# The first chunk's attention in fixed slots on TensorE

## The chip, the cores and the metric

One Trainium2 chip, of which the kernel uses one core. The metric is the device time of one execution in microseconds (us). The kernel before took 813.23 us as the median of three runs (812.15 to 815.35).

## The reference

Attention whose queries and keys meet only where a hash of both is the same, followed by two feed-forward layers:

```python
# q, k, v: (2, 8, 768, 64); proj: (64, 6)
q_bits = (einsum('bhsd,dk->bhsk', q, proj) > 0)
k_bits = (einsum('bhsd,dk->bhsk', k, proj) > 0)
mask = q_bucket[:, :, :, None] == k_bucket[:, :, None, :]
scores = where(mask, q @ k.T / sqrt(64), -1e9)
attn = exp(scores - max); attn /= sum(attn) + 1e-9
x = heads joined of attn @ v                   # (1536, 512)
h = maximum(x @ w_in, 0);  x = (h * h) @ w_out     # first layer, d_ff 2048
h = x @ w_in2; x = (maximum(h, 0) + alpha * minimum(h, 0)) @ w_out2
```

The weights arrive as float64 bits and are converted to float32 on the chip.

## The kernel before, in words

The 1536 rows are cut into four chunks of 384 (T). The attention of chunk 0 runs alone at the start (`attention(0, 2)`); that of chunks 1 to 3 (`attention_beside`) runs in the background of the first layer's matmuls (`feed_forward`) of chunks 0 to 2. The second layer follows (`wide_hidden`, `whole_project`).

In a chunk the eight heads go in four pairs (`Pair`), one head in each half of the partitions. A pair has six units: head h, query block t of 128 rows. `scores` (L382) makes four matmuls into a buffer of `s_tile` (two buffers, `s` and `acc`, that alternate), DVE takes the maximum of 768 scores (`low`, L393) and ACT the exponent with its sum (`sm`, L396). `p_t` (L403) transposes the result on TensorE, three key blocks to a bank of `m_tile`, and evicts it to `pt` on ACT (L415) or DVE (L417), by the letters of `EVICT`. `av` (L419) multiplies six key blocks by the values, two matmuls (one per head, each into half of the columns) a block; the trace shows two records for each of these. `recip` (L437) turns the sums into a row and spreads it over the partitions by way of DRAM, or, for the last pair of chunk 0, by matmuls (`spread`, L461); `finish` (L471) multiplies and splits into a high and a low part for the feed-forward layer.

A pair is prepared while the one before runs: `k_bits` and `q_split` hash on TensorE (L239), `matches` compares hash codes on TensorE (L255), `k_split` makes high and low parts of the keys, `k_ids` makes the key row that is zero where a code matches (L279, DVE), and two DMAs each bring these into the tile `k` (L275, L285). `q_halves` (L306) and `q_yes` (L326) do the same for the queries. The first pair is prepared in one piece, `at_once` (L331).

In chunk 0 `m_tile` hands out three PSUM banks in turn (two of `ps_m` and `ps_h`), for transposes, hashes, matches and products alike. `pt` has two buffers, one for each head of a pair, so that a pair's first transposes wait for the products of the pair before. In the order of the program, two preparation steps follow each score group, and the six blocks of products follow the last transposes of a pair. That order is only a priority: a planner lists the instructions of each engine by what it takes to be ready first. `tc.keep_in_program_order` binds an instruction to the written order on its engine; before, `Pair.next` used it for some instructions of the first two pairs. Behind the attention of chunk 0, `fetch` converts the first feed-forward weights (DVE L617, L618, L623; ACT L615), allowed to begin after the last unit of pair 2.

Of the kernel before, what the change touches and what calls it, by code (L numbers as in the profile page):

```python
# [17 lines left out]
NEG = -(2.0 ** 100)  # L18
# [11 lines left out]
def kernel(  # L30
# [64 lines left out]
    p2 = pool("p2", 2, att)  # L95
    p4 = pool("p4", 4, att)
    sm3 = pool("sm3", 3, att)

# [31 lines left out]
    pop = const.tile([P, 1], F32, name="pop")  # L130
    off = const.tile([P, 1], F32, name="off")

    def constants():
# [3 lines left out]
        with tc.tile_pool(name="once", bufs=1) as once:  # L137
# [32 lines left out]
            first(nc.vector.tensor_scalar(off, pop, -1.0, 1.0, ALU.mult, ALU.add))  # L170
# [35 lines left out]
    class Pair:  # L206
# [26 lines left out]
        def hash_bits(self, x, n):  # L233
# [4 lines left out]
            for g in range(NG):  # L238
                self.next(nc.tensor.matmul(  # L239
# [6 lines left out]
        def matches(self, bits, n):  # L246
# [6 lines left out]
            for g in range(NG):  # L253
                a, k = divmod(g * w, T)
                nc.tensor.matmul(ps[:, a, k:k + w], code[:, g, :], bits, start=True, stop=True)  # L255
# [35 lines left out]
        def q_split(self):  # L291
# [6 lines left out]
            self.q3 = p1.tile([P, 3, T], F32R, tag="q3", name="q3")  # L298
# [17 lines left out]
        def q_ids(self):  # L316
# [4 lines left out]
            nc.scalar.activation(self.q3[:, 0], y[:, 0, :], AF.Relu, bias=off)  # L321
# [4 lines left out]
        def q_yes(self, y):  # L326
            for h in range(2):
                r, o = self.rows(h)
                self.next(nc.scalar.activation(self.q[o, h, 0], y[r, 0, :], AF.Relu, bias=off[r]))

        def at_once(self):  # L331
# [10 lines left out]
            for h in range(2):  # L342
                self.next(nc.scalar.activation(q[r[h], h, 0], self.qn[r[h]], AF.Copy, scale=scale))
            nc.gpsimd.tensor_copy(k[r[0], 0, 1], f32(k[r[0], 0, 0]))
            nc.gpsimd.tensor_copy(q[o[0], 0, 1], f32(q[r[0], 0, 0]))
            nc.sync.dma_start(out=f32(k[r[1], 1, 1]), in_=f32(k[r[1], 1, 0]))
            nc.sync.dma_start(out=f32(q[o[1], 1, 1]), in_=f32(q[r[1], 1, 0]))
            k_y = self.matches(k_bits, S)
            for h in range(2):
# [136 lines left out]
    def attention(c, lag):  # L486
# [33 lines left out]
        while late:  # L520
            tail()
# [688 lines left out]
```

## Time and profile before

| | us |
|---|---|
| median of three runs | 813.23 |
| lowest, highest | 812.15, 815.35 |
| profiled execution | 814.07 |
| its span | 812.3 |
| TensorE matmuls busy | 773.7 (95%) |
| DVE, ACT, GpSimd busy | 541.5, 507.1, 317.1 |

The profile is of one execution. Busy is the time in which an engine has an instruction under way; a matmul's record includes the time until its results are out, so that records that follow each other overlap. "idle before <- releaser" is the time for which an engine did nothing ahead of an instruction and the work that ended that wait. Times of a row count from the span's start.

### The profile page before, as it was taken

To read this page: it belongs to the slowest core of one execution; us is meant where nothing else is said; L and a number is where in the kernel's file an instruction comes from. 1 tells how busy PE (TensorE), PEld (TensorE's weight loads), DVE (VectorE), ACT (ScalarE), POOL (GpSimd) and SP (SyncE) were. 2 spreads that over 40 slices of the span, in tenths; PEclk is the share of its full clock that TensorE was granted. 3 is DMA by queue.
4 is the path that set the end of the run, shared out by engine and by line. 5 is a ranking of instruction groups with operands and counts; after the bars stand their busy time and mean duration, and the time that the engine had idled before them with its cause. 6 is when DMAs were issued, how large, how long until landed. Compare 5 with 4: busy or idle time off the path is not lost.

```text
span 812.3 us, 12536 instructions
## 1 busy us (share of the span) xinstructions
PE 773.7 (95%) x4330; PEld 634.4 (78%) x4330; DVE 541.5 (67%) x876; ACT 507.1 (62%) x988; POOL 317.1 (39%) x231
## 2 busy tenths in 40 slices
PE   6899899999999998999999999999999999999998
PEld 4565777766778676676867769999999888999886
DVE  8578899887756657788977964574667622766111
ACT  5678778767565555565756656775777633777331
POOL 1012322233346464654343342002558354558440
PEclk9999999999999999999999999999999999999999
DMA  6856878778678586768785657451321226511222
GB/s 179 216 160 207 270 244 253 240 218 247 167 247 237 178 246 216 249 231 272 221 268 160 223 198 284 123 162 44 133 71 53 56 68 206 193 58 57 65 65 91
DMA packets 56708, 143.67 MB, mean 177 GB/s; under 512 B 7402, under 2 KB 11652, under 8 KB 56644
## 3 DMA queue, kind: packets, MB, share of 16 engines
q1 hardware_dynamic: 56644, 142.87, 56.4%
q8 instruction: 34, 0.56, 0.3%
q14 instruction: 30, 0.25, 0.1%
HBM read 96.62 MB, written 25.47 MB: 150 GB/s over the span
## 4 chain that ended last, share of the span: by engine, by line
PE 47%; DVE 4%; DMA 3%; issue 1%; ACT 1%; ACTq 0%; DVEq 0%
PE b L1036 5%; PE b L1037 5%; PE b L1042 5%; PE b L903 5%; PE b L902 5%; PE b L904 5%; DMA wf<-w 3%; PE m L427 2%; PE s L388 1%; PE h L706 1%; PE h L707 1%; PE h L708 1%; PE m L411 1%; PE acc L751 1%; PE acc L747 1%
## 5 line engine op out<-in xcount | busy, mean ns | idle before, releaser
L668 POOL TENSOR_TENSOR wl<-wf,wh 128x512 fp32r<-128x512 f32 x64 | 88.6, 1387 | 80.4 <-ACT wh L667 74.8
L939 POOL TENSOR_TENSOR wp<-wraw,wp 128x1024 fp32r<-128x1024 f32 (+1 forms) x32 | 68.3, 2136 | 117.7 <-ACT wp L936 96.0
L667 ACT ACTIVATE wh<-wf 128x512 fp32r<-128x512 f32 x128 | 79.8, 628 | 54.4 <-PE h L707 23.1
L396 ACT ACTIVATE sm<-s,low 128x768 f32<-128x768 f32 x84 | 75.6, 900 | 49.4 <-DVE low L393 49.2
L719 POOL TENSOR_TENSOR gl<-g,gh 128x384 fp32r<-128x384 f32 x48 | 54.6, 1137 | 128.9 <-ACT g L716 65.0
L393 DVE TENSOR_REDUCE low<-s 128x1 f32<-128x768 f32 x84 | 80.0, 952 | 31.0 <-PE s L388 30.8
L388 PE MATMUL s<-k,q 128*128 128x384 f32 x336 | 80.8, 360 | 10.7 <-ACT sm L396 9.5
L411 PE MATMUL m<-ident,sm 128*128 128x128 f32 x531 | 85.3, 277 | 5.9 <-DVE pt L417 3.3
L411 PEld LDWEIGHTS m<-ident,sm 128*128 128x128 f32 x531 | 65.4, 142 | 24.1 <-DVE pt L417 4.9
L1026 POOL TENSOR_TENSOR gp<-g,gp 128x768 fp32r<-128x768 f32 x32 | 63.2, 1981 | 50.5 <-ACT gp L1023 50.5
L388 PEld LDWEIGHTS s<-k,q 128*128 128x128 f32 x336 | 58.2, 193 | 27.8 <-ACT sm L396 17.5
L706 PE MATMUL h<-xh,wh 128*128 128x384 f32 x212 | 77.2, 364 | 2.1 <-DVE u L474 1.7
L1036 PE MATMUL b<-wp,gp 128*128 128x512 f32 x192 | 75.0, 391 | 0.0
L904 PE MATMUL b<-xph,wp 128*128 128x384 f32 x224 | 74.8, 334 | 0.0
L902 PE MATMUL b<-xph,wp 128*128 128x384 f32 x224 | 74.8, 334 | 0.0
L903 PE MATMUL b<-xpl,wp 128*128 128x384 f32 x224 | 74.8, 334 | 0.0
L1037 PE MATMUL b<-wp,gp 128*128 128x512 f32 x192 | 74.8, 389 | 0.0
L708 PE MATMUL h<-xh,wl 128*128 128x384 f32 x212 | 71.9, 339 | 0.3 <-POOL wl L668 0.3
L707 PE MATMUL h<-xl,wh 128*128 128x384 f32 x212 | 71.7, 338 | 0.0
L668 DVE TENSOR_TENSOR wl<-wf,wh 128x512 fp32r<-128x512 f32 x64 | 48.2, 757 | 31.2 <-ACT wh L667 31.2
L1020 DVE TENSOR_TENSOR wp<-wp 128x512 fp32r<-128x512 f32 x28 | 25.4, 911 | 64.0 <-ACT wp L1017 64.0
L427 PE MATMUL m<-pt,vr 128*64 128x384 f32 x336 | 66.2, 498 | 1.5 <-DVE rrow L445 0.9
(180 smaller groups left out, 1824.4 us busy)
## 6 DMA issues: line engine op xcount, KB each, us to landing
wf<-w SPq DMA_DIRECT2D x96, 256.0 KB, 3.1
wbits<-in_w_in_dram SPq DMA_DIRECT2D x32, 512.0 KB, 4.3
wbits<-in_w_out_dram SPq DMA_DIRECT2D x32, 512.0 KB, 4.0
wraw<-ws SPq DMA_DIRECT2D x16, 896.0 KB, 4.7
q<-q SPq DMA_DIRECT2D x48, 192.0 KB, 3.9
w<-wf SPq DMA_DIRECT2D x32, 256.0 KB, 2.2
wp<-w SPq DMA_DIRECT2D x32, 256.0 KB, 2.6
k<-kh SPq DMA_DIRECT2D x14, 384.0 KB, 6.3
```

The source lines that it names most:

```text
L388: nc.tensor.matmul(ps[:, a, 0:HALF], self.q[:, h, i, qs], self.k[:, h, i, ks], start=i == 0, stop=i == 1)
L393: low_ins = nc.vector.tensor_reduce(low, ps[:, 0:2, 0:HALF], AX.XY, ALU.max, negate=True)
L411: nc.tensor.transpose(ps[:, i * P:(i + 1) * P], pp[:, b * P:(b + 1) * P], ident)
L427: nc.tensor.matmul(self.o[r, 0:T], self.vr[:, b, r], self.pt[h][:, :, b, :], start=(b == 0), stop=(b == NKB - 1),)
L668: engine.tensor_tensor(lo, w, f32(hi), ALU.subtract)
L706: nc.tensor.matmul(hp, wih[:, ks], xh[:, kk, :], start=first, stop=False)
L708: nc.tensor.matmul(hp, wil[:, ks], xh[:, kk, :], start=False, stop=last)
L902: nc.tensor.matmul(ps, w[0][:, ms], gh, start=first, stop=False, skip_group_check=True)
L903: nc.tensor.matmul(ps, w[0][:, ms], gl, start=False, stop=False, skip_group_check=True)
L904: nc.tensor.matmul(ps, w[1][:, ms], gh, start=False, stop=last, skip_group_check=True)
L1036: nc.tensor.matmul(a, g[:, 0, b], w[:, 0], start=f == 0, stop=False)
L1037: nc.tensor.matmul(a, g[:, 0, b], w[:, 1], start=False, stop=False)
```

## The change

For chunk 0 the steps are written out by `attention_first` in 24 slots. Slot n holds the scores of unit n, one step of the next pair's preparation (in pair 0 from the second slot on), the transposes of unit n - 2 (and the sums' row after a pair's last), and key blocks of the products of the pair before: one block in slot 1, two in slots 2 and 3, one in slot 4; `finish` of that pair is in slot 5. After the last slot the last pair's products follow in three groups of two blocks. All matmuls of chunk 0's attention are bound to this order (`Pair.pe`). The products take `ps_h` (`h_tile`) and all else the two banks of `ps_m`. `pt` has a third buffer (`third`), used for every third head; its memory later serves `y` and the second chunk's `q3`. The key row becomes 0 or -1 (a sign on ACT in the first pair, in `at_once`, with the order of the steps there changed; DVE elsewhere), and the factor 2^100 goes to the query's row.

```diff
     def m_tile():
         state["m"] += 1
-        if not state["moe"] and state["m"] % 3 == 0:
-            return ps_h.tile([P, 512], F32, tag="h", name="h")
         return ps_m.tile([P, 512], F32, tag="m", name="m")
...
+        def pe(self, ins):
+            if self.c == 0:
+                tc.keep_in_program_order(ins)
...
-                self.kr[:, 0].bitcast(F32R).rearrange("p (a n) -> p a n", n=T), y, pop, NEG,
+                self.kr[:, 0].bitcast(F32R).rearrange("p (a n) -> p a n", n=T), y, pop, -1.0,
                 ALU.not_equal, ALU.mult,
...
-            self.q3 = p1.tile([P, 3, T], F32R, tag="q3", name="q3")
+            self.q3 = state["q3"].tile([P, 3, T], F32R, tag="q3", name="q3")
...
-            for h in range(2):
-                self.next(nc.vector.tensor_tensor(k[o[h], h, 1], kr[r[h]], f32(k[r[h], h, 0]), ALU.subtract))
-                if h == 0:
-                    self.q_yes(self.matches(self.hash_bits(self.qn, T), T))
-                self.next(nc.vector.tensor_scalar(
-                    k[o[h], h, 0].rearrange("p (a n) -> p a n", n=T), k_y[r[h]], pop[r[h]], NEG,
-                    ALU.not_equal, ALU.mult,
-                ))
...
+            def ids(h):
+                self.next(nc.scalar.activation(
+                    k[o[h], h, 0].rearrange("p (a n) -> p a n", n=T), k_y[r[h]], AF.Sign, bias=npop[r[h]]
+                ))
...
+            low("k", 0)
+            q_bits = self.hash_bits(self.qn, T)
+            q_y = self.matches(q_bits, T)
+            ids(0)
+            self.next(nc.scalar.activation(q[r[1], 1, 0], self.qn[r[1]], AF.Copy, scale=scale))
             nc.sync.dma_start(out=f32(q[o[1], 1, 1]), in_=f32(q[r[1], 1, 0]))
+            low("q", 0)
+            yes(0)
+            ids(1)
+            low("k", 1)
+            low("q", 1)
+            yes(1)
...
-                self.pt[h] = p2.tile([P, NTB, NKB, P], F32, tag="pt", name="pt")
+                by = "third" if self.c == 0 and (2 * self.j + h) % 3 == 2 else "p2"
+                self.pt[h] = state[by].tile([P, NTB, NKB, P], F32, tag="pt", name="pt")
...
-            if part == 0:
-                self.o = m_tile()
             n = NKB // 3
-            for b in range(part * n, (part + 1) * n):
+            self.blocks(part * n, (part + 1) * n)
+
+        def blocks(self, b0, b1):
+            if b0 == 0:
+                self.o = h_tile() if self.c == 0 else m_tile()
+            for b in range(b0, b1):
...
+    def attention_first():
+        units, lag = 2 * NTB, 2
+        pairs = [Pair(0, j) for j in range(NPAIR)]
+        for step in pairs[0].prepare():
+            step()
+        prep = []
+
+        def turn(n):
+            pr, u = pairs[n // units], n % units
             for a in range(2):
+                pr.p_t(*divmod(u, NTB), a)
+            if u == units - 1:
+                pr.recip()
+
+        parts = {1: (0, 1), 2: (1, 3), 3: (3, 5), 4: (5, 6)}
+        for n in range(NPAIR * units):
+            j, u = divmod(n, units)
+            if u == 0 and j + 1 < NPAIR:
+                prep = pairs[j + 1].prepare()
+            pairs[j].scores(*divmod(u, NTB))
+            if prep and (u or j):
+                prep.pop(0)()
+            if n >= lag:
+                turn(n - lag)
+            if j and u in parts:
+                pairs[j - 1].blocks(*parts[u])
+            if j and u == units - 1:
+                pairs[j - 1].finish()
+            assert not (prep and u == units - 1)
+        for n in range(NPAIR * units - lag, NPAIR * units):
+            turn(n)
+        for b in range(0, NKB, 2):
+            pairs[-1].blocks(b, b + 2)
+        pairs[-1].finish()
...
     state["moe"] = True
+    passing.close()
+    state["y"] = pool("y", 1, layer1, side="right")
+    state["q3"] = pool("q3", 1, passing, side="right")
     wide_banks.close()
```

## Rows read from the trace of the kernel before

**Rows 1.** Busy time by stage: length, engines (instructions), clock, DMA share, GB/s.

```profile
core 0: us, PE busy (x) PEld busy (x) DVE busy (x) ACT busy (x) POOL busy (x), PEclk, DMA share, GB/s
8.40:24.90 16.50, 13.55 (x73) 10.04 (x73) 12.62 (x17) 10.51 (x21) 1.77 (x2) 1.00 0.73 174
24.90:43.10 18.20, 16.62 (x114) 10.44 (x112) 12.12 (x21) 11.72 (x27) 1.62 (x2) 1.00 0.66 182
43.10:60.40 17.30, 16.05 (x108) 10.38 (x108) 12.21 (x21) 12.91 (x29) 2.07 (x3) 1.00 0.69 187
60.40:74.20 13.80, 13.21 (x76) 8.54 (x76) 11.68 (x22) 11.23 (x25) 2.85 (x2) 1.00 0.58 180
74.20:86.00 11.80, 8.91 (x62) 5.16 (x62) 11.34 (x22) 8.77 (x18) 3.22 (x5) 1.00 0.74 259
86.00:497.00 411.00, 392.61 (x2262) 302.41 (x2262) 316.08 (x512) 262.31 (x532) 168.87 (x139) 1.00 0.74 231
```

**Rows 2.** Waits of TensorE, 86 to 497 us: sum, times, longest.

```profile
PE s L388 <- ACT sm L396: 6.9, 8, 1.8
```

**Rows 3.** Waits of ACT and DVE, 24.8 to 60.3 us: sum, times, longest.

```profile
ACT u L435 <- PE m L427: 4.8, 1, 4.8
ACT u L435 <- PE h L427: 4.3, 1, 4.3
...
DVE low L393 <- PE acc L388: 7.1, 5, 3.7
```

**Rows 4.** TensorE's timeline, slots without products: start, length, instruction, count.

```profile
58.68 0.94 PE L388 MATMUL acc<-k,q 128*128 128x384 f32 x4
...
60.35 0.97 PE L388 MATMUL s<-k,q 128*128 128x384 f32 x4
61.16 0.82 PE L411 MATMUL m<-ident,sm 128*128 128x128 f32 x6
61.99 0.97 PE L388 MATMUL acc<-k,q 128*128 128x384 f32 x4
...
70.02 0.82 PE L411 MATMUL m<-ident,sm 128*128 128x128 f32 x6
70.60 0.94 PE L388 MATMUL acc<-k,q 128*128 128x384 f32 x4
```

**Rows 5.** TensorE's timeline, the last pair's products and what follows each group.

```profile
78.92 2.80 PE L427 MATMUL m<-pt,vr 128*64 128x384 f32 x16 [0.34 <-ACT pt L415]
81.65 0.93 PE L465 MATMUL h<-rrow,pick 6*128 6x128 f32 x6
82.51 1.51 PE L427 MATMUL m<-pt,vr 128*64 128x384 f32 x8
83.95 0.37 PE L239 MATMUL m<-qn,proj_sb 128*32 128x96 f32 x8
```

**Rows 6.** TensorE's timeline, a pair's key hash and key matches.

```profile
25.74 0.53 PE L239 MATMUL h<-kr,proj_sb 128*32 128x192 f32 x8
...
46.64 0.49 PE L255 MATMUL acc<-bits,code 128*128 128x192 bf16 x4
```

**Rows 7.** Timelines of DVE, ACT and TensorE in the first 18 us.

```profile
9.87 1.02 DVE L353 TENSOR_SCALAR k<-s,pop 64x768 fp32r<-64x768 f32 x1
...
12.50 0.90 ACT L396 ACTIVATE sm<-acc,low 128x768 f32<-128x768 f32 x1 [3.53 <-DVE low L393]
...
15.94 1.48 PE L388 MATMUL s<-k,q 128*128 128x384 f32 x4
```

**Rows 8.** Pair 1's key identities, issue on SP; landing times of that line.

```profile
16.29 2.45 SPq L285 DMA_DIRECT2D k<-kr  x2
...
DMA to landing us min/median/max: 4.8/5.9/7.1
```

**Rows 9.** Timelines at the end of the stage: last scores, last multiplication, first feed-forward matmul.

```profile
74.19 0.96 PE L388 MATMUL acc<-k,q 128*128 128x384 f32 x4
...
85.38 0.55 DVE L474 TENSOR_TENSOR u<-u,h 128x384 f32<-128x384 f32 x1
...
85.98 0.44 PE L706 MATMUL h<-xh,wh 128*128 128x384 f32 x1 [1.66 <-DVE u L474]
```

More of the change, by code (lines that the diff above doesn't have):

```diff
@@ L94 @@
     p1 = pool("p1", 1, att)
-    p2 = pool("p2", 2, att)
+    p2 = state["p2"] = pool("p2", 2, att)
     p4 = pool("p4", 4, att)
     sm3 = pool("sm3", 3, att)
+    passing = ctx.enter_context(ExitStack())
+    state["third"] = pool("third", 1, passing, side="right")
     def s_tile():
@@ L169, in constants @@
             first(nc.vector.tensor_reduce(pop, ones, AX.X, ALU.add))
-            first(nc.vector.tensor_scalar(off, pop, -1.0, 1.0, ALU.mult, ALU.add))
+            first(nc.vector.tensor_scalar(npop, pop, -1.0, None, ALU.mult))
+            first(nc.vector.tensor_scalar(off, pop, -FAR, FAR, ALU.mult, ALU.add))
     xT = {}
@@ L238, in hash_bits @@
             for g in range(NG):
-                self.next(nc.tensor.matmul(
+                self.pe(nc.tensor.matmul(
                     ps[g * GR:(g + 1) * GR, 0:w], proj_sb.rearrange("p h n -> p (h n)"), x[:, g * w:(g + 1) * w],
@@ L320, in q_ids @@
                 return
-            nc.scalar.activation(self.q3[:, 0], y[:, 0, :], AF.Relu, bias=off)
+            nc.scalar.activation(self.q3[:, 0], y[:, 0, :], AF.Relu, bias=off, scale=FAR)
             for h in range(2):
@@ L328, in q_yes @@
                 r, o = self.rows(h)
-                self.next(nc.scalar.activation(self.q[o, h, 0], y[r, 0, :], AF.Relu, bias=off[r]))
+                self.next(nc.scalar.activation(self.q[o, h, 0], y[r, 0, :], AF.Relu, bias=off[r], scale=FAR))
         def at_once(self):
@@ L341, in at_once @@
                 self.next(nc.scalar.activation(k[r[h], h, 0], kr[r[h]], AF.Copy))
-            for h in range(2):
-                self.next(nc.scalar.activation(q[r[h], h, 0], self.qn[r[h]], AF.Copy, scale=scale))
             nc.gpsimd.tensor_copy(k[r[0], 0, 1], f32(k[r[0], 0, 0]))
+            nc.sync.dma_start(out=f32(k[r[1], 1, 1]), in_=f32(k[r[1], 1, 0]))
+            self.next(nc.scalar.activation(q[r[0], 0, 0], self.qn[r[0]], AF.Copy, scale=scale))
             nc.gpsimd.tensor_copy(q[o[0], 0, 1], f32(q[r[0], 0, 0]))
-            nc.sync.dma_start(out=f32(k[r[1], 1, 1]), in_=f32(k[r[1], 1, 0]))
@@ L347, in at_once @@
[L347 to L359 removed]
+            k_y = self.matches(k_bits, S)
@@ new lines, in yes @@
+            def yes(h):
+                self.next(nc.scalar.activation(
+                    q[o[h], h, 0], q_y[r[h], 0, :], AF.Relu, bias=off[r[h]], scale=FAR
+                ))
+            low("k", 0)
[3 more added lines that the diff above has]
+            self.next(nc.scalar.activation(q[r[1], 1, 0], self.qn[r[1]], AF.Copy, scale=scale))
+            nc.sync.dma_start(out=f32(q[o[1], 1, 1]), in_=f32(q[r[1], 1, 0]))
+            low("q", 0)
@@ L484, in new_x @@
         return xT[key]
-    def attention(c, lag):
-        def begin():
-            if (c, 0) not in raw:
-                load_pair(c, 0)
-        pairs = [Pair(c, j) for j in range(NPAIR)]
-        steps = [begin] + pairs[0].prepare()
-        late = []
-        ended = []
-        def tail():
-            pr, h, t = late.pop(0)
-            for a in range(2):
-                steps.append(lambda a=a: pr.p_t(h, t, a))
-            if t == NTB - 1 and h == 1:
-                steps.append(pr.recip)
-                for part in range(3):
-                    steps.append(lambda part=part: pr.av(part))
-                ended.append(pr)
-        for j, pr in enumerate(pairs):
-            nxt = pairs[j + 1].prepare() if j + 1 < NPAIR else []
-            for u in range(2 * NTB):
-                h, t = divmod(u, NTB)
-                steps.append(lambda pr=pr, h=h, t=t: pr.scores(h, t))
-                late.append((pr, h, t))
-                for _ in range(2 if c == 0 else 1):
-                    if nxt:
-                        steps.append(nxt.pop(0))
-                if ended and u == 3:
-                    steps.append(ended.pop().finish)
-                if len(late) > lag:
-                    tail()
-        while late:
-            tail()
-        while ended:
-            steps.append(ended.pop(0).finish)
-        return steps
@@ L1055 @@
     constants()
-    for step in attention(0, 2):
-        step()
+    attention_first()
     with tc.issue_after(keyed[0, 1].ins):
```

38 lines of the change are left out of this document (22 added, 16 removed).

## The prediction

> **What bounds the kernel now.** I read four views, in this order. First the busy time by stage [rows 1], cut where the attention of the first chunk passes from one head pair to the next. Call its 24 score groups n0 to n23: six per pair, one for each head and each block of 128 query rows. n0 starts at about 8.4, n6 at 24.9, n12 at 43.1, n18 at 60.4, n23 at 74.2, and the first feed-forward matmul at 86.0 us. So the stage that the diff rewrites takes 77.6 us, a tenth of the span. Behind it, from 86 to 497 us, TensorE is busy 392.6 of 411.0 us, and its longest kind of wait sums to only 6.9 us [rows 2]: there TensorE's work sets the pace, and a microsecond won before 86 should arrive at the end. In the stage itself DVE and ACT are busy 12 to 13 of some 18 us per pair. Neither is the bound as an average, and TensorE's 16 of 17 to 18 is not either, since its records overlap and include matmuls that run at the wrong time.
>
> What is wrong there shows in the second and third view. TensorE runs the products of a whole pair (24 records, two per matmul) nearly in one piece, and while it does so no new scores come. ACT waits 4.8 and 4.3 us in single stretches for the end of those products, and DVE waits 7.1 us for scores, all between 24.8 and 60.3 us [rows 3]. The fourth view, TensorE's timeline, gives the prices of its pieces: scores take 0.81 us from their start to the next instruction, six transposes 0.57 [rows 4], 16 product records 2.73 and 8 records 1.44 [rows 5].
>
> **The change, part by part, and its sum.** The sum is made against the profiled execution: 814.07 us, of which 812.3 is the span and 1.77 lies around it; this execution is 0.84 above the median of the three, 813.23.
>
> *Slots for pairs 1 and 2.* A slot is now fixed: scores, one step of the next pair's preparation, the six transposes of two slots back, and zero, one or two of the six key blocks of the pair before. TensorE's work for a pair is six times 0.81 + 0.57, 8.28 us. For the products, 16 records (four key blocks) cost 2.73 and 8 records (two blocks) 1.44, so a block costs 0.645 and each group a fixed 0.15; six blocks in four groups (1, 2, 2, 1) cost 4.47. The preparation: the key hash 0.53 and the key matches 0.49 [rows 6]; the query's two have half the columns, so they lie between nothing and these, and I take 0.4 together, towards the upper row since short matmuls do not shrink in proportion. The transposed sums, 0.2 by the same reasoning. In all 14.4 us. On the other side stands the loop through two score buffers: n17 at 58.68, n19 in the same buffer at 61.99, so 3.31 us for two slots [rows 4], 9.9 us for six, which lies below 14.4 and so does not bind on average. It binds in the slots without products (the last of a pair and the first of the next): they have 1.4 to 1.9 us of TensorE work where the loop wants 1.65, and ACT has there the exponent and two query rows of the next pair ahead of evictions. I add 1.1 us a pair for that, between nothing and 2.2. So 15.5 against 18.2 and 17.3 [rows 1]: 2.7 and 1.8 us won.
>
> The products become more groups, and here a rule of the Trainium skill speaks against the change: "TensorEngine Tiling (Array Packing)", Key Properties, says that a change of tiling mode drains TensorE, and the products use a 128 by 64 mode among 128 by 128 matmuls. The trace has the drain in its numbers: the fixed 0.15 us of a group, which makes four groups 0.45 dearer than one. By the rule alone nothing more is due, and the sum holds it.
>
> *The third transposed tile and the bank of its own for products.* They let the first transposes of a pair be written before the products of the pair before have ended. They add no instruction. The price: transposes, hashes and matches lose one of three PSUM banks. I cost that at nothing, because scores (0.81) and products (1.44) stand between two uses of a bank and cover an eviction; where the cover is gone, it is the rival "slower" below.
>
> *Pair 3.* It has no preparation, so n18 to n23 is five times 1.38 plus 4.47 plus 0.2, 11.6 us; with 0.8 us of waits 12.4 against 13.8: 1.4 won.
>
> *The start.* DVE made both key rows of the first pair (1.02 us each), so that ACT waited 3.53 us for the first minimum and started the exponent at 12.50 [rows 7]. Signs on ACT take two 1 us pieces off DVE while ACT waits, so the first exponent can come about 1.1 us sooner. But the preparation of pair 1 now goes one step to a slot, beginning at slot 1, and its key identities stand behind n3 instead of n1. Before, the transfers that bring them were issued from 16.29 for 2.45 us, landing 4.8 to 7.1 us after an issue [rows 8], and n6 came at 24.9. After: n0 at 8.4; scores here run at half speed (1.48 for four in the record at 15.94 [rows 7] against 0.97 for those at 60.35 [rows 4]); three scores, a hash and six transposes at that speed and one wait for an exponent put n3 at about 15.7 us. Its own 1.5, the matches, DVE's minimum and the 1 us identities follow: 19.5. Two issues, which no longer wait behind DVE, 1.2 (half of 2.45): 20.7. Landed at 25.5 to 26.6, and I take 26.0. TensorE keeps its order, so it stands still from about 23 to 26 with n6 at the head of its queue and the transposes of slots 4 and 5 behind it. 1.1 us lost, between 0.5 won and 2.6 lost. In pairs 2 and 3 the identities stand in slot 2, four slots ahead of their scores: some 10 us against the 9 that the same chain takes, so these should just land in time.
>
> *The tail.* Scores, transposes and products behind n23 are the same work in the same order. The first feed-forward matmul waited for the bank of which the last multiplication read (85.38, 0.55 long, behind weight conversions) [rows 9]; that bank now comes free with the copy of the products, about 1 us sooner, but the last third of that group still needs the last pair's columns. 0.8 won, between 0.3 and 1.5.
>
> *Smaller edits.* The query tile of the second chunk waits for the third tile's memory, so one activation and one DVE operation move from idle time near 50 us to about 70, where DVE is fuller: hidden by the tail's 11 us of products, half a microsecond if not. Its DMAs follow on SP, well ahead of their use after 86. The scale and bias edits change values, not durations.
>
> Sum: +1.1 - 2.7 - 1.8 - 1.4 - 0.8 = -5.6; the profiled execution would take 808.4, and the median 0.84 less, 807.6.
>
> **The rivals.** *Keys come late* in all three boundaries. For: slack of only 1 us at n12 and n18, and landing times that spread by 2.3 us [rows 8]. Price: 2.6 instead of 1.1 at n6 and 1.5 at each of the others, 4.5 more: 812.1. TensorE would stand still for three or four us each time; after 20 us no wait of the trace of before is that long, so it does not show whether the clock holds through one. By the difference 1.48 to 0.97 each score group at the lower level costs 0.5 more, some 2 us in all if one boundary ends so; I give that a third of this rival's chance, and it would end at 814. The Trainium skill, "TensorE: Matmul & The Clock Gate", section "HAM oscillation — how this bites in real kernels", describes that case, waits for transfers between bursts that bring the lower clock back.
>
> *The gain is given back.* The weights of the first chunk are converted on DVE beside the last pair and the tail: DVE is busy 11.7 of 13.8 and 11.3 of 11.8 us [rows 1]. With attention 5 us shorter, less conversion is done by the first feed-forward matmul, and DVE is three quarters busy on average behind it. Against: DVE's idle time before 60 us is what the slots use up, and TensorE has hardly any wait there. Full return: 812.5.
>
> *Slower.* An eviction on ACT's queue stands behind an exponent that waits for DVE, and TensorE, with two banks and a fixed order, stops at the next transposes, and all that is behind them stops too. n0 to n23 took 65.8 us before, 2.86 a slot; my sum gives 61.4, 2.67. So the point from which it decides is 0.2 us more wait per slot; at 0.4 the kernel loses 4.4 us: 817.7, at half the exponent's 0.9 in each slot 819. Before, the planner could put any ready matmul into such a hole.
>
> *No change in kind.* The planner's order was worth as much as the fixed one: 813.
>
> **How the numbers follow.** Chances: the forecast 0.55, keys late 0.13, given back 0.14, slower 0.13, no change 0.05. The forecast's own range: with no added waits (3.0 less) and the early key landing (1.6 less) 803.0; with the waits doubled (3.0 more) and the late landing (1.5 more) 812.1. About half a per cent, 4.1 us, is what a measurement of this kernel can tell from no change, so faster means under 809.2 and slower over 817.3. Of the forecast's 0.55, 0.49 lies under 809.2. Faster 0.49; same 0.06 + 0.13 + 0.14 + 0.05 and a little of the slower rival, 0.40; slower 0.11. The range 803.5 to 814.5 holds nearly all of the forecast, the late keys, the return and no change, and leaves out the slower rival and the forecast's lowest end, under 2 in 10.
>
> **What would show it.** In the profile of after: single waits of 4 us of ACT for the end of the products gone; scores every 2.3 to 2.8 us through pairs 1 and 2; n6 at about 26 with a wait on transfers just before it (if it is at 24 or sooner, the key step is wrong); n12 near 41.5, n18 near 57, n23 near 69.4; the first feed-forward matmul near 80.5; and the same 726 us from there to the end as before. If waits of scores or transposes on ACT or DVE sum to over 8 us in the stage, the slower rival holds; if the first feed-forward matmul comes early but the rest is longer, the return.

## The result and the profile after

The changed kernel took 821.62 us (median of 6 runs, 819.04 to 827.57), the kernel before beside it 813.22: 1.0105 times as long, interval 1.0065 to 1.0144. The forecast was 807.6 and its range ended at 814.5. The profiled execution of after is 823.46 us with a span of 821.7; 812.3 before. Executions of one kernel differ by some microseconds: 31 of the kernel before, beside e1 to e4 below, took 809.8 to 818.31. A profile shows one of them.

Of the 9.4 us, 7.3 are in the stage: the first feed-forward matmul starts at 93.25 instead of 85.98. The other 2.1 lie behind it. First the busy time by stage of after, cut at its own n6, n12, n18, n23 and first feed-forward matmul, to be read against [rows 1]:

```profile
core 0: us, PE busy (x) PEld busy (x) DVE busy (x) ACT busy (x) POOL busy (x), PEclk, DMA share, GB/s
8.40:24.80 16.40, 12.06 (x73) 9.10 (x73) 11.74 (x19) 12.28 (x26) 1.72 (x3) 1.00 0.56 137
24.80:44.30 19.50, 15.86 (x108) 9.86 (x109) 10.41 (x17) 11.91 (x25) 0.89 (x1) 1.00 0.77 201
44.30:65.80 21.50, 17.76 (x112) 10.92 (x111) 11.93 (x21) 11.71 (x27) 2.58 (x3) 0.92 0.67 198
65.80:80.00 14.20, 12.58 (x79) 8.22 (x77) 13.33 (x25) 13.07 (x28) 2.26 (x2) 1.00 0.48 143
80.00:93.30 13.30, 10.94 (x68) 5.86 (x66) 11.48 (x21) 7.54 (x16) 3.50 (x5) 0.87 0.61 193
93.30:504.30 411.00, 391.73 (x2238) 301.36 (x2235) 314.85 (x509) 259.25 (x525) 167.25 (x138) 0.98 0.74 228
```

The first pair is as long as before, 16.4 for 16.5; each of the others is longer: 19.5 for 18.2, 21.5 for 17.3, 14.2 for 13.8. TensorE's idle time in a pair is the length less its busy time: 3.6, 3.7 and 1.6 us here, 1.6, 1.25 and 0.6 in [rows 1]. The clock, 1.00 in every stretch before, shows 0.92 in the second pair and 0.87 in the tail.

What ends TensorE's idle time, summed over the whole stage (sum, times, longest), after and then before:

```profile
PE m L473 <- DVE rin L471: 3.8, 3, 1.6
PE m L437 <- DVE bits L250: 3.4, 4, 2.0
PE m L437 <- ACT pt L441: 2.3, 5, 1.0
PE m L437 <- ACT q L336: 1.8, 2, 0.9
PE s L413 <- DMA k<-kr: 1.4, 1, 1.4
```

```profile
PE s L388 <- ACT sm L396: 2.6, 4, 1.6
PE h L706 <- DVE u L474: 1.7, 1, 1.7
```

The new waits are not of scores (L413). They are of transposes (L437) that want a bank of `ps_m` whose last occupant a slower engine has not read yet: a key hash (`bits`), a query match (`q` L336), an earlier transpose (`pt`). And they are of the sums' row (L473), which stands in the fixed order before its reciprocal is made. How such a wait comes about, in TensorE's and DVE's timelines (start, length, instruction, idle before and releaser):

```profile
24.76 0.94 PE L413 MATMUL s<-k,q 128*128 128x384 f32 x4 [1.38 <-DMA k<-kr]
25.63 0.53 PE L246 MATMUL m<-kr,proj_sb 128*32 128x192 f32 x8
26.09 0.55 PE L437 MATMUL m<-ident,sm 128*128 128x128 f32 x3
28.68 0.55 PE L437 MATMUL m<-ident,sm 128*128 128x128 f32 x3 [2.04 <-DVE bits L250]
28.98 0.95 PE L413 MATMUL acc<-k,q 128*128 128x384 f32 x4
...
50.75 0.27 PE L473 MATMUL m<-ident,rin 128*6 128x128 f32 x1 [1.63 <-DVE rin L471]
50.95 1.28 PE L457 MATMUL h<-pt,vr 128*64 128x384 f32 x4
52.16 1.65 PE L413 MATMUL acc<-k,q 128*128 128x384 f32 x4
```

```profile
26.82 0.56 DVE L319 SCALAR_TENSOR_TENSOR q<-qn,q 64x384 fp32r<-64x384 f32 x1 [2.31 <-ACT q L317]
27.40 0.96 DVE L418 TENSOR_REDUCE low<-s 128x1 f32<-128x768 f32 x1
28.28 0.35 DVE L250 TENSOR_SCALAR bits<-m 128x192 bf16<-128x192 f32 x1
```

The hash at 25.63 takes one bank and three transposes at 26.09 the other. The next three need the hash's bank, which DVE reads only at 28.28, behind a query row that waited 2.31 for ACT and behind a minimum. The scores of the next slot, for which nothing was missing, stand behind those transposes until 28.98.

Behind two such waits the clock falls. Busy time and granted clock around the one at 50.75:

```profile
49.00:51.00 2.00, 0.37 (x5) 0.13 (x3) 1.38 (x4) 0.99 (x2) 0.00 (x0) 1.00 0.00 0
51.00:53.00 2.00, 2.00 (x8) 0.99 (x8) 0.28 (x1) 0.00 (x0) 0.00 (x0) 0.57 0.16 43
53.00:55.00 2.00, 2.00 (x12) 1.66 (x11) 1.16 (x2) 0.00 (x0) 0.00 (x0) 0.58 0.95 338
```

The score group at 52.16 takes 1.45 us to the next start, where one at full clock takes 0.81 [rows 4]. The same follows the row of the last pair at 85.58 (waited 1.12): 0.60 and 0.55 from 85 to 89. At the lower level (1.2 of 2.4 GHz) the two falls cost up to 3.4 us, half of the time spent there.

### The profile page after: what moved, and what is told of

Its sections match the earlier page's. It is cut to its first block, busy times and chain, and to the rows that moved or that the text cites. A ratio compares the mean times of both kernels' runs of the same rounds, so it can differ in the third digit from the quotient of the medians.

```text
span 821.7 us, 12535 instructions
## 1 busy us (share of the span) xinstructions
PE 777.3 (95%) x4330; PEld 636.8 (78%) x4330; DVE 539.5 (66%) x875; ACT 511.1 (62%) x990; POOL 316.6 (39%) x231
## 4 chain that ended last, share of the span: by engine, by line
PE 74%; DVE 10%; ACT 6%; DMA 5%; issue 3%; POOL 1%; SPq 0%; DVEq 0%; ACTq 0%; POOLq 0%
PE b L1062 5%; PE b L1063 5%; PE m L457 5%; PE s L413 5%; PE b L1068 5%; PE b L930 5%; PE b L928 5%; PE b L929 5%; PE m L437 4%; PE h L732 3%; PE h L733 3%; PE h L734 3%; PE acc L777 3%; PE acc L773 3%; PE acc L774 2%
## 5 line engine op out<-in xcount | busy, mean ns | idle before, releaser
L694 POOL TENSOR_TENSOR wl<-wf,wh 128x512 fp32r<-128x512 f32 x64 | 86.9, 1360 | 90.2 <-ACT wh L693 72.6
L437 PE MATMUL m<-ident,sm 128*128 128x128 f32 x576 | 93.6, 279 | 11.7 <-DVE bits L250 5.7
L437 PEld LDWEIGHTS m<-ident,sm 128*128 128x128 f32 x576 | 71.3, 142 | 32.0 <-DVE bits L250 7.3
L413 PE MATMUL s<-k,q 128*128 128x384 f32 x336 | 78.3, 354 | 10.2 <-ACT sm L421 7.7
L413 PEld LDWEIGHTS s<-k,q 128*128 128x128 f32 x336 | 57.6, 190 | 26.5 <-ACT sm L421 15.4
L443 DVE COPY pt<-m 128x384 f32<-128x384 f32 x104 | 56.9, 549 | 20.2 <-PE m L437 19.9
L773 PE MATMUL acc<-wh,gh 128*128 128x512 f32 x144 | 66.0, 458 | 0.0
```

Of the source, the lines that this page charges most:

```text
L413: self.pe(nc.tensor.matmul(ps[:, a, 0:HALF], self.q[:, h, i, qs], self.k[:, h, i, ks], start=i == 0, stop=i == 1))
L437: self.pe(nc.tensor.transpose(ps[:, i * P:(i + 1) * P], pp[:, b * P:(b + 1) * P], ident))
L694: engine.tensor_tensor(lo, w, f32(hi), ALU.subtract)
L773: nc.tensor.matmul(acc[t], gh[:, blocks[t]], woh, start=first, stop=False)
```

## The experiments

Each edit is against the changed kernel unless it says otherwise; `+` and `-` lines alone. None leaves any work out. "First activation" is that of the first feed-forward matmuls.

**One remedy at a time.** Four edits, one for each part that could carry the waits: where the preparation stands, the lost bank, where the row stands, and the binding itself.

`e1_prep_behind`: the preparation step behind the transposes of its slot.

```diff
-            if prep and (u or j):
-                prep.pop(0)()
             if n >= lag:
                 turn(n - lag)
+            if prep and (u or j):
+                prep.pop(0)()
```

> One edit on the changed kernel: in each slot of the first chunk the preparation step (key or query hash, or matches) stands behind the six transposes instead of ahead of them. Theory A, banks held: with two banks, a hash or a match ahead of the transposes keeps one bank until DVE has read the bits or ACT the query row, and the second half of the transposes stops for it; the profile after has 3.4 us of such waits on the bits and 1.8 us on the query row in the stage, and 0.5 to 2.3 us more behind each than the wait itself. It expects these to go, the first feed-forward matmul at 86 to 89 us instead of 93.3, and 814 to 818 us instead of 821.6. Theory B, fixed order as such: TensorE stops wherever the head of its queue is not ready, and the waits move to the next slot; within 2 us of 821.6. Theory C, behind the stage: the loss is made by falls of the clock after 93 us; within 2 us of 821.6 whatever the stage does.

816.63 us, 1.0041 (1.0014 to 1.0068). That is in the range of theory A. The waits of transposes on `bits` and on `q` L336 are gone, and others stand in their place:

```profile
PE s L413 <- ACT q L317: 4.1, 1, 4.1
PE m L437 <- ACT pt L441: 3.8, 5, 1.0
```

`e2_third_bank`: three banks for transposes, hashes and matches again; the products get a bank that a smaller score tile leaves free.

```diff
-            return ps_a.tile([P, 3, 512], F32, tag="acc", name="acc")
+            return ps_a.tile([P, 2, 512], F32, tag="acc", name="acc")
...
+        if not state["moe"] and state["m"] % 3 == 0:
+            return ps_h.tile([P, 512], F32, tag="h", name="h")
...
-                self.o = h_tile() if self.c == 0 else m_tile()
+                self.o = ps_a.tile([P, 512], F32, tag="o", name="o") if self.c == 0 else m_tile()
```

> One edit on the changed kernel: transposes, hashes and matches of the first chunk get their third bank back, and the products take a bank that the three-bank score tile left unused (that tile now has two). Theory A, banks held: all waits of transposes on the bits (3.4 us), the query row (1.8 us) and evictions (2.3 us) in the stage shrink to under 1.5 us together; the first feed-forward matmul at 84 to 87 us, 811 to 816 us in all. The waits of the sums' row on DVE's reciprocal (3.8 us) stay. Theory B, fixed order as such: the waits stay within a third, 818 to 823 us. Theory C: the stage shortens but the total stays within 2 us of 821.6.

815.72 us, 1.0017 (0.9996 to 1.0038): 5.9 us of the 8.4 come back, as theory A has it; by the intervals that can't be told from what the other three edits give. Transposes no longer wait for hashes, matches or evictions, and two other waits come out in full:

```profile
PE s L415 <- DMA k<-kr: 4.7, 1, 4.7
PE h L475 <- DVE rin L473: 4.3, 2, 2.6
```

The first is that of n6, at 25.89: the late key transfer that the prediction put at 26.0. The clock averages 0.57 from 23 to 31. This execution, 818.02 us, is the longest of its ten.

`e3_row_later`: the sums' row one slot later, to leave DVE time for its reciprocal.

```diff
+        def recip_row(self):
...
             pairs[j].scores(*divmod(u, NTB))
+            if j and u == 2:
+                pairs[j - 1].recip_row()
...
             pairs[-1].blocks(b, b + 2)
+            if b == 0:
+                pairs[-1].recip_row()
```

> One edit on the changed kernel: the transposed sums of a pair stand one slot later on TensorE (behind the next scores; for the last pair behind its first two key blocks), while DVE's reciprocal keeps its place. Theory A2, one more holder of the fixed order: TensorE waits 3.8 us in three places for that reciprocal, and the clock falls to its lower level right behind two of them (at 50.8 and 85.6 us). It expects these waits under 1 us, no fall of the clock there, and 4 to 7 us less: 815 to 818. Theory B: the wait moves to the next instruction, since DVE is late anyway: within 2 us of 821.6.

817.0 us, 1.0042 (1.0015 to 1.0068). That is in the range of theory A2. No wait on `rin`, and no fall of the clock at 51 and 85; but in this execution the clock falls from 24 to 32 instead, around n6, for as long as the two falls of after together. The waits for banks remain (`pt` 4.1 us in 7, `bits` 1.9, `q` 1.8).

`e4_free_order`: the same order of the program, but TensorE is not bound to it (the hashes of the first two pairs alone stay bound, as before).

```diff
-            if self.c == 0:
-                tc.keep_in_program_order(ins)
+            return ins
...
-                self.pe(nc.tensor.matmul(
+                self.next(nc.tensor.matmul(
```

> One edit on the changed kernel: the matmuls of the first chunk are no longer bound to the written order; the planner places them, with the same slots as a priority, two banks and the third transposed tile (the first two pairs' hashes stay bound as they were before). Theory B, fixed order as such: the holes are filled, the first feed-forward matmul comes at 80 to 86 us, 806 to 814 us. Theory A, banks held: with two banks the planner has little to put there and TensorE still takes its instructions in one order: 816 to 823 us. Here the two are furthest apart.

816.88 us, 1.003 (1.0006 to 1.0054). The planner fills the holes: the longest wait of the stage is 1.9 us, and the first activation comes at 87.13, 1.6 us sooner than before (88.73). So the stage does what theory B expected, with the first feed-forward matmul at 84.11. Yet the time is theory A's, and the kernel is not faster than before. Behind the stage (85 to 500 us) scores wait longer than the 6.9 of [rows 2]:

```profile
PE s L412 <- ACT sm L420: 10.1, 10, 2.8
```

So each of the four gives back 4.6 to 5.9 us. They are not four separate losses: two of them together (e5, below) give back only 3.5. And in the three that stay bound, only 3.4, 2.5 and 1.2 us lie ahead of the first activation (92.70, 93.68 and 94.91 for 96.14 in after); behind it after has four falls of the clock, e1 and e3 none and e2 one.

**Remedies together.** `e5_bank_row` is the edits of e2 and e3, `e7_bank_free` those of e2 and e4. `e8_bank_row_keys` adds to e5 that the second pair's preparation begins in the first slot, two steps at a time:

```diff
-            if prep and (u or j):
-                prep.pop(0)()
+            for _ in range(1 if j else 2):
+                if prep:
+                    prep.pop(0)()
```

> On the changed kernel both edits together: the third bank for transposes, hashes and matches (products in the spare bank of the score tile), and the sums' row one slot later. Theory A, single holders of the fixed order (bank, row): what each alone gave back (5.9 us the bank, 4.6 us the row) adds up for the most part; the waits of TensorE in the stage fall under 8 us, no fall of the clock at 50 us, 811 to 813.5 us. Theory D, one lateness behind them all: DVE and ACT are late in the slots without products and TensorE meets this at whatever stands next in its order; then the two do not add up, and the total stays at 815 to 817.

> On the changed kernel the third bank and the planner's order: of the change remain the slots as priorities, the third transposed tile, the bank of its own for products and the signs. Theory B (the fixed order loses, the rest gains): the first feed-forward activation comes at 82 to 86 us (88.7 in the kernel before), 809 to 812 us. Theory E (what is won in the stage is given back behind it, as with the free order and two banks, which reached its first feed-forward activation 1.6 us ahead of the kernel before and ended 1.9 us behind it): 813.5 to 817 us although the stage is shorter.

> As the third bank with the row one slot later, and the second pair's preparation begins in slot 0 with two steps to a slot, as the kernel before had it. Theory K (the late keys cost on their own): with the third bank the seventh score group waited 4.7 us for its keys and the clock was at its lower level from 24 to 31 us; with the keys asked for two slots sooner that wait falls under 1 us, the clock holds, the seventh score group starts at 22 to 23.5 us, and the total is 2 to 5 us under the same kernel without this edit. Theory D (DVE and ACT late at the boundary anyway): under 1.5 us less.

e5 818.11 us, 1.0076 (1.005 to 1.0102); e7 819.47, 1.0078 (1.0043 to 1.0113); e8 817.32, 1.006 (1.0035 to 1.0084). The times of e5 and e7 lie above the ranges of both their theories, and e8 is only 0.8 us under e5. But the stage does what the change was meant to do. Bank and row together (e5) bring the first activation to 87.38, 8.8 us sooner than in after and 1.4 sooner than before: these two carry the loss of the stage. In e8 the key identities are issued from 15.42 instead of 18.46, no wait on a transfer is left at n6 (23.9), and every part of the stage is shorter than in [rows 1] (the same columns as above; the tail follows below):

```profile
8.40:23.90 15.50, 10.79 (x72) 8.33 (x72) 10.94 (x16) 11.70 (x24) 1.50 (x2) 1.00 0.77 187
23.90:41.00 17.10, 15.86 (x109) 10.20 (x110) 11.09 (x20) 12.08 (x27) 1.01 (x2) 1.00 0.68 178
41.00:57.90 16.90, 15.66 (x113) 10.27 (x111) 12.14 (x21) 11.69 (x27) 2.02 (x3) 1.00 0.72 197
57.90:71.00 13.10, 12.81 (x77) 8.29 (x75) 12.14 (x22) 12.02 (x27) 1.74 (x2) 1.00 0.61 215
```

Its first feed-forward matmul starts at 80.83, 5.2 us sooner than before and close to the 80.5 of the forecast. But that matmul reads columns of earlier pairs; the first activation needs those of the last pair too and gains only 2.7 us (86.05 for 88.73). TensorE's, DVE's and ACT's timelines of e8, and below them the copy of the last products in the kernel before:

```profile
79.39 1.51 PE L459 MATMUL o<-pt,vr 128*64 128x384 f32 x8
80.83 0.44 PE L745 MATMUL h<-xh,wh 128*128 128x384 f32 x1
```

```profile
81.01 1.40 DVE L656 TENSOR_SCALAR wsg<-wbits 128x512 uint32<-128x512 uint32 x1
82.44 0.69 DVE L657 SCALAR_TENSOR_TENSOR wsg<-wbits,wsg 128x512 uint32<-128x512 uint32 x1
83.05 0.55 DVE L512 TENSOR_TENSOR u<-u,m 128x384 f32<-128x384 f32 x1
```

```profile
81.58 0.49 ACT L467 ACTIVATE u<-o 128x384 f32<-128x384 f32 x1
...
86.05 0.47 ACT L752 ACTIVATE r<-h 128x384 f32<-128x384 f32 x1
```

```profile
84.13 0.49 ACT L435 ACTIVATE u<-m 128x384 f32<-128x384 f32 x1
```

The last products end 3.1 us sooner than before (80.83 for the 83.95 of [rows 5]); the other 2.0 of the 5.2 are time that the first feed-forward matmul spent behind them, chiefly its wait on `u`, and that the last columns do not gain. The last multiplication stands on DVE behind two pieces of weight conversion, but 0.98 us after the end of the copy `u`, where it was 0.76 before: little is given back there. The gain that is left, 2.7 us, goes behind the first activation, where the longest sum of waits (85 to 500 us) is:

```profile
PE s L415 <- ACT sm L423: 10.4, 8, 2.8
```

**The signs alone.** `e9_signs_alone` is the kernel before with only the sign rows, the scales and the new `at_once`:

```diff
-                self.next(nc.vector.tensor_scalar(
-                    k[o[h], h, 0].rearrange("p (a n) -> p a n", n=T), k_y[r[h]], pop[r[h]], NEG,
...
+                self.next(nc.scalar.activation(
+                    k[o[h], h, 0].rearrange("p (a n) -> p a n", n=T), k_y[r[h]], AF.Sign, bias=npop[r[h]]
...
```

> The kernel before with one part of the change alone: the first pair's key rows by sign on ACT and the new order of its preparation. By the prediction's step for the start the first exponent begins at 11.4 instead of 12.5 us, the seventh score group 1 us sooner, and 0.5 to 1.5 us are won: 812 to 813 us beside 813.4. The rival: the start is followed by waits on the second pair's keys and on exponents that do not move, and nothing comes through: within 0.5 us of the kernel before.

812.76 us, 0.9996 (0.997 to 1.0021): no gain and no part of the loss that the runs can tell, although its first activation comes at 87.15, 1.6 us sooner.

**The order behind the stage.** The planner lists the background work of chunks 1 to 3 anew for every program; in after 95% of TensorE's records behind the stage stand in the order of before, in e8 91%, in e9 all (the share that lies in common runs of the two sequences). Six kernels bind a recorded order behind the stage on all engines, each instruction to the one that it follows:

```diff
+    for engine, order in stored_order().items():
...
+        for one, two in zip(order, order[1:]):
+            tc.add_manual_dep(
+                mine[two], mine[one].name,
+                mybir.DependencyInfo(mybir.DependencyClass.NoSync, mybir.DependencyReason.DATA),
...
```

`f0_before_own_order` is the control, the kernel before with its own order; `f1_e8_order_before` is e8 with the order of before, `f2_before_order_e8` the kernel before with that of e8, `f3_after_order_before` the changed kernel with that of before. `f4_e8_order_late` and `f5_after_order_late` bind the order of before only from the first copy of chunk 0's result on.

> The kernel before, with its own order of instructions behind the first chunk's attention bound on every engine, as in the three kernels that bind an order; nothing else is changed. Theory A, binding an order costs nothing by itself: 812 to 813.5 us, ratio 0.998 to 1.002, chunk 0 to chunk 2 in about 261 us, as in the kernel before. Rival B, binding takes something away or adds waits by itself: over 815, and the longer times of the kernels with exchanged orders say nothing of the orders.

> The kernel with the third bank, the later row and the earlier keys, whose stage ended 2.7 us sooner than in the kernel before (first feed-forward activation at 86.05 against 88.73 us) but which took 817.3; behind the stage its instructions now stand on all engines in the order that the planner gave the kernel before (a stored list; the stage itself is left to the planner as it was). Theory P (the planner's order behind the stage took the gain): the time behind the first activation goes from 727.8 back to about 724, the waits of score groups on exponents from 10.4 to about 7 us, and the total is 808.5 to 811.5, under the kernel before. Theory S (an earlier start is itself given back, by weights and keys that are not ready): 815 to 818 as without the list.

> The opposite: the kernel before, stage untouched, with the order behind the stage that the planner gave the kernel of the third bank, later row and earlier keys. Theory P: its stage stays at 88.7 us, but it loses 3 to 5 us behind it: 816 to 819. Theory S: the order behind the stage does not matter: 812 to 814.

> The changed kernel as it is, with the order of the kernel before behind the stage. By the traces the changed kernel lost 7.4 us up to the first feed-forward activation and 2.0 behind it, the latter with four falls of the clock against one. Theory P: the 7.4 us stay, the 2 us behind it go: 819 to 820.5. Theory S: within 1 us of 821.6. If the order behind the stage carried most of the loss after all: under 817.

> The kernel e8_bank_row_keys with the order of the kernel before bound on every engine only from the first copy of chunk 0's feed-forward result on; the order before that point is left to the planner. Theory A, the order of chunk 1 to chunk 3's background work carries the loss: from the first copy of chunk 0 to the last copy of chunk 2 about 261 us instead of 264 to 270, end of chunk 0 at about 228.5 as in e8, so some 814 us, ratio 1.000 to 1.003. Rival B, the order of the background and the end of the stage belong together, so that the bound order meets other transfers and buffers: 817 or more, with new waits of TensorE behind 228 us.

> The changed kernel with the order of the kernel before bound from the first copy of chunk 0's feed-forward result on. Theory A: the stage keeps its loss (first feed-forward matmul at about 93, first activation at about 96, end of chunk 0 at about 237), and chunk 0 to chunk 2 takes about 261 us against the 263.0 of the changed kernel: 819 to 820 us. Rival B, the bound order costs waits of its own: 823 or more.

The stretches of the profiled executions, in us: to the first activation, from there to DVE's first copy of chunk 0's result (in e5, e8, f2 and f4 a copy on ACT came 0.9 to 1.4 us ahead of it), from there to the last copy of chunk 2's, from there to the end; and TensorE's time at the lower clock (twice what the granted clock of each microsecond lacks of 1.00, without the last few, where TensorE has ended). Each row is one execution, for e2 and e5 the longest of ten, for e1 the second shortest (813.99 to 820.29); differences of a few microseconds between rows may be the execution's and not the kernel's.

| | ratio (interval) | to first | chunk 0 | chunks 1, 2 | rest | span | low clock |
|---|---|---|---|---|---|---|---|
| before | 1 | 88.7 | 139.3 | 260.9 | 323.4 | 812.3 | 3.4 |
| after | 1.0105 (1.0065 to 1.0144) | 96.1 | 141.5 | 263.0 | 321.1 | 821.7 | 20.5 |
| e1 | 1.0041 | 92.7 | 135.9 | 262.5 | 321.1 | 812.2 | 6.8 |
| e2 | 1.0017 | 93.7 | 137.9 | 261.7 | 322.9 | 816.2 | 13.7 |
| e3 | 1.0042 | 94.9 | 138.0 | 260.4 | 320.7 | 814.0 | 6.8 |
| e4 | 1.003 | 87.1 | 138.3 | 266.6 | 322.2 | 814.2 | 6.8 |
| e5 | 1.0076 | 87.4 | 140.3 | 268.6 | 325.0 | 821.3 | 20.5 |
| e7 | 1.0078 | 88.3 | 140.5 | 267.3 | 321.4 | 817.5 | 13.6 |
| e8 | 1.006 | 86.1 | 142.5 | 264.2 | 321.1 | 813.8 | 6.8 |
| e9 | 0.9996 | 87.2 | 139.3 | 261.2 | 323.8 | 811.4 | 10.3 |
| f0 | 0.9998 (0.9973 to 1.0022) | 89.9 | 139.3 | 259.6 | 324.2 | 813.0 | 10.2 |
| f1 | 1.007 (1.0045 to 1.0094) | 87.6 | 145.5 | 261.6 | 323.7 | 818.4 | 17.1 |
| f2 | 1.0143 (1.0111 to 1.0175) | 89.4 | 141.0 | 270.4 | 321.6 | 822.3 | 17.1 |
| f3 | 1.0185 (1.0151 to 1.0219) | 98.9 | 144.8 | 259.4 | 323.8 | 826.9 | 23.9 |
| f4 | 1.0138 (1.01 to 1.0176) | 85.9 | 142.2 | 269.7 | 324.0 | 821.8 | 20.5 |
| f5 | 1.0135 (1.0096 to 1.0174) | 95.2 | 141.0 | 261.5 | 323.2 | 820.9 | 13.6 |

f0 (813.22 us beside 812.09) shows that binding an order costs nothing by itself that could be told. f2 (823.94 beside 812.22, more than either theory gave it) shows that the order matters: with an unchanged stage, the order of e8 makes chunks 1 and 2 take 270.4 instead of 260.9, and the kernel 1.4% longer. But the order of before does not save the others. In f1 (818.54) and f3 (827.8) chunks 1 and 2 take 261.6 and 259.4 again, as before, and the feed-forward of chunk 0 becomes 145.5 and 144.8: the bound scores of chunk 1 now reach TensorE before their queries have been brought. First f1's wait, then f3's:

```profile
PE s L453 <- DMA q<-q: 3.2, 1, 3.2
```

```profile
PE s L451 <- DMA q<-q: 2.4, 1, 2.4
```

f4 (823.94) was to keep e8's own first 140 us; there the seam itself, the point from which the order is bound, stops TensorE, and the clock averages 0.57 from 240 to 252 us:

```profile
244.75 0.69 PE L774 MATMUL h<-xh,wh 128*128 128x384 f32 x1 [7.04 <-ACT r L781]
```

So f4 can't say what that order would be worth without the seam. f5 (823.7) had chunks 1 and 2 in 261.5, 1.5 less than after, and gave 2.1 back in the rest. In all four a bound order that was listed for another stage made the kernel no faster; that an order is good only for the times at which its own stage ends is what this suggests, and no run here shows it.

## Why the prediction was wrong

The profiled execution was to take 808.4 and took 823.5, 15.1 us more. By the terms of the sum:

| | predicted | measured | difference |
|---|---|---|---|
| n6 | 26.0 | 24.76 | -1.2 |
| n6 to n12 | 15.5 | 19.58 | +4.1 |
| n12 to n18 | 15.5 | 21.48 | +6.0 |
| n18 to n23 | 12.4 | 14.18 | +1.8 |
| n23 to first feed-forward matmul | 11.0 | 13.25 | +2.3 |
| behind it, to the end of the span | 726.3 | 728.45 | +2.1 |

**The step that failed** is the price of the third bank, "I cost that at nothing, because scores (0.81) and products (1.44) stand between two uses of a bank and cover an eviction". In a slot with a hash or a query match that is not so: hash and six transposes use the two banks three times within the slot, with only three transposes between (25.63, 26.09 and 28.68 above). And a bank that holds a hash comes free not by an eviction, but when DVE reaches `bits` in its queue. e2 gives the third bank back, and with it the waits of transposes on `bits`, `q` and `pt` and 5.9 us go.

**A second step** is the "1.1 us a pair" of added waits: TensorE idled 3.6 and 3.7 us, and 1.6 instead of 0.8 in pair 3. Of it the row's wait, 3.8 us in the three that the stage shows, was in no term: I gave the transposed sums 0.2 us of work and did not ask when DVE makes their reciprocal (for the row at 50.75 only at 50.41, behind an eviction and a query row). e3 moves the row; its waits and the two falls behind them go, and 4.6 us.

**A third step** is "a microsecond won before 86 should arrive at the end". With the first two mended (e8) the stage is what the forecast wanted, the first feed-forward matmul at 80.83 for 80.5, and yet the kernel takes 817.32 us, not 807.6.

**The work term** was nearly right. Its pieces are as costed: four product records take 0.80 to the next start (31.04 to 31.84), where the sum had 0.645 + 0.15. The fixed 0.15 us a group is there again, and no dearer. The prediction put it down to the drain that the Trainium skill, "TensorEngine Tiling (Array Packing)", Key Properties, gives for a change of tiling mode; that it is the drain, no run here shows. TensorE was busy 15.9 us in the first of the two pairs instead of 14.4. An estimate of the rest: a stop also shows the end of the record before it, 0.55 us for three transposes instead of the 0.3 to the next start in a stream (26.09 and 28.68), so the four stops of that pair show 1.0 us.

**The keys.** The identities were issued from 18.46, not 19.5: n3 starts at 14.26, not 15.7, since TensorE is at full speed by then (the scores at 12.20 take 1.65, those at 14.26 0.94), where the prediction kept half speed. Against that the two issues took 2.69 us, not 1.2. n6 started at 24.76 after a wait of only 1.38, since two stops before it (0.58 and 0.97 on `pt`) had used up the rest. Where those stops are gone (e2) it waits 4.7 us and starts at 25.89. So the 26.0 of the forecast was met within 1.2 us, in part by two errors that offset each other. At n12 and n18 the keys landed in time, as forecast. The rival of late keys at all three boundaries is out.

**Start, tail, what lies behind.** The first exponent came at 11.15 instead of 12.50, 1.35 sooner for a forecast of 1.1. The wait of the first feed-forward matmul on `u` (1.7 before) is gone, as forecast, but the row's wait of 1.12 and the fall of the clock behind it cost more. "The same 726 us behind" held to 2.1 us in after, but as a rule it is refuted: in e4, e5 and e8 the stage gives 1.4 to 2.7 us in the profiled execution, and the median lies 3.5 to 5.6 us behind that of the kernel before.

**The rivals.** *Slower* was the right one, at a chance of 0.13. n0 to n23 took 71.5 us, 3.11 a slot. The terms of the sum add up to 61.0 us for that, 2.65 a slot (the prediction has 61.4 and 2.67), so a slot took 0.46 more, and the point from which this rival decides was 0.2. At 0.4 it gave 817.7. Its sign came too: scores and transposes waited 9.9 us for ACT and DVE in the stage, over the 8 that it named. Its place was half right: the transposes stood still, but more for hashes and matches (5.2 us) than for evictions (2.3). *The gain is given back* did not come by its mechanism in after, which had no gain to give. In e8 the gain was given back, but not by the weight conversions that this rival named. By the profile the 2.7 us of the first activation are lost in chunk 0, which takes 3.2 longer (waits on exponents of 4.1 instead of 2.7, a fall of the clock from 155 to 159), and chunks 1 and 2 take 3.3 longer, while the rest is 2.3 shorter; the prediction named no mechanism for that.

**What stays open** is why e8 ends 4 to 5 us behind the kernel before. That the order of the background work can cost that much is shown (f2); how much of e8's loss is the order's, and why the planner's order for e8 has more waits on exponents, is not. No kernel here kept both, a stage as short as e8's and chunks 1 and 2 as short as before. Part of it may be the clock: the median granted clock of e8's ten executions is 0.992, of the kernel before beside them 0.996, an estimated 3.3 us at most of the 4.8; but the record of the clock leaves out the start (see the last section), so this is not settled.

## What to carry to other kernels

Before an engine is bound to a written order, list for every slot how many buffers of each pool it takes, who frees each, and what stands ahead of that instruction in its own queue: a buffer read late stops not its next user alone but all that is written behind it, ready or not. A planner that may reorder is worth what the trace shows it doing with ready work in such holes; here binding four kinds of instruction to two banks cost more than the stray products that it removed. And a stage made shorter in front of planned background work need not pay, even where the planner lists that work anew for the earlier start, as in e8: measure the end, not the stage, and over several executions.

## What the runs showed of the chip

The time goes with TensorE's clock. In the profiled executions, one of each kernel, the seven kernels with up to 10.3 us at the lower level have spans of 811.4 to 814.2 us, the nine with 13.6 us or more 816.2 to 826.9. The 20.5 us of after are worth up to 10.2 us of full clock, the 3.4 of before up to 1.7. The record of the clock begins only at 18.5 us in before and at 13.7 in after; ahead of it the rows show 1.00, but the pieces take the times of the lower level (the hash at 11.33 in after 0.87 us, as at 27.44 in e2 at 0.50). So before was at the lower level some 4.8 us longer there, and the gap between the two kernels is smaller by that.

The other executions agree: the six of after took 819.04 to 820.09 us at a mean granted clock of 0.992, 823.15 at 0.990, 823.46 at 0.988 and 827.57 at 0.986. An estimate from the median clocks, with the span times what the clock lacks of 1.00 as the most that it cost: 7.4 us in after (0.991), 2.9 in e3 (0.9965), 5.7 in e2 (0.993). So what the moved row gives back (4.6) can be the clock alone, and what the third bank gives back (5.9) is for the most part the waits themselves.

Each fall in after begins at the end of a single wait of TensorE, or within 1 us behind it: at 50.75 (1.63 us), 85.58 (1.12), 225.71 (2.96), 330.41 (2.34), 344.72 (2.05) and 368.21 (2.27). The length of the wait alone does not decide: the wait of 2.04 at 28.68 was followed by no fall. That the falls cause the longer spans, and do not only go along with the waits, is argued from the score group of 1.45 us for 0.81 and from the executions above; no run tried it by itself.

The prediction had this only for waits on transfers, as "TensorE: Matmul & The Clock Gate" of the Trainium skill tells it in "HAM oscillation — how this bites in real kernels". Here the trace agrees for the transfer (e2, 4.7 us, a mean of 0.57 from 23 to 31 us), but most falls came behind waits of 1 to 3 us on DVE and ACT.
